# Block-recurrent cross attention and an ELU layer pair on one core: a second Strassen level for P1, softmax steps on GpSimd, later transposes

## The chip, the cores and the metric

One Trainium2 chip, of which the kernel uses one core. The metric is the device time of one execution in microseconds: the median of the runs shown. A core has five instruction queues: PE (TensorE, matmuls, with its weight loads counted apart as PEld), DVE (VectorE), ACT (ScalarE), POOL (GpSimd) and SP (SyncE, here the issuer of nearly all DMAs). Each runs its own queue in order; semaphores tie them together.

## The reference

The inputs are x (8 batches, 8 heads, 512 rows, 64 columns), state (8, 8, 32, 64), w_in (512 by 2048) and w_out (2048 by 512), all float32. Attention goes both ways between x and state, and the result feeds two dense layers with an ELU between them:

```python
scores = scale * np.matmul(x, state.transpose(0, 1, 3, 2))   # softmax over the 32 states -> a
xread = np.matmul(a, state)
scores2 = scale * np.matmul(state, x.transpose(0, 1, 3, 2))  # softmax over the 512 rows -> a2
sread = np.matmul(a2, x)
...
h = x @ w_in                                                 # x: all 4352 rows of [xread, sread]
g = np.where(h > 0.0, h, alpha * (np.exp(np.minimum(h, 0.0)) - 1.0))
return (g @ w_out).astype(np.float32)
```

## The kernel before, in words

**Stages.** Batches 0 and 1 run first (`start()`), while the weights are read and converted; `ffn2_1` ends batch 1; then `batch(b)` runs for b = 2 to 7, and `states()` does the 256 state rows of all batches and the last stores. In the steady part a batch has two halves. The first half is the expansion: four chunks (`ffn1_chunk`) of 512 of the 2048 hidden columns. The transposed softmax weights `a_sb` (128 by 1024) are multiplied with M = state x w_in (`make_m`, from w_in blocks fetched back from DRAM, copied out of PSUM by ACT in `copy_m`). Each chunk is a Strassen-Winograd product: seven products of 128x256 tiles (`two`) instead of eight. Its left sums are made by POOL (`sum_m`), its right sums too (`sum_a`), and `elu` turns the results into `g_sb`. `elu` has two forms: by ACT (exp, relu on ACT, one combining step on DVE) or by DVE (exp on ACT, a tensor_scalar and a max on DVE).

The second half is the contraction g x w_out (`ffn2`), again Strassen-Winograd with seven products P1 to P7. Six of them (P2, P4, P6, P7, P5, P3 in this order) are split once more, by the class `Second`: `sums` makes four sums of g blocks on DVE (128x512 each), and `steps` runs seven products of four 128x128 matmuls each, every one followed by a copy (ACT) or an accumulation (DVE) of a 128x128 block into `ob`. The weight sums of the second level are made once, in `weights`, and `restore` undoes the one of them made in place. P1 alone is plain: 16 matmuls of 128x256 (`product`), and one ACT copy.

**The next batch** is prepared within this one. `load_blocks` brings x of batch b+1 into `ob` (16 DMAs of 64 KB, once `ob`'s former contents are stored), `turn_blocks` transposes it on DVE into `xr` (four instructions of 128x512), `scores` multiplies it with the state. `softmax` makes `a_sb`: transpose, row maximum, subtract, exp, sum, multiply by the reciprocal, transpose. `softmax_rows` makes the weights of the other direction, `move_state` transposes them and moves them across partitions with 16 DMAs, and `state_read` multiplies them with x (`load_x`).

**What sets the order.** Every operation is recorded in a plan (`Plan.add`) with an assumed cost and its dependences. `Plan.run` then goes through the operations engine by engine: PE takes the first ready operation in the written order, the others the ready one that is due first, POOL keeps the written order. DMAs have an assumed rate and landing time (`DMA_COST`, `LANDING`). The order that comes out is fixed in the program. `plan.behind(op)` makes operations wait for `op`, except POOL's. All instructions are issued through one helper, so the profile shows nearly all of them with one line, L463; the groups are told apart by tile names: `ps` is PSUM, `m`, `s` and `aT` hold M and the right factors (and serve as sums' places in the second half), `g` the hidden values, `sec` and `t_w` sums and weights of the second level, `w_half` w_in blocks, `xe` and `xr` the next batch's data, `o` the output and the blocks of the next x.

Of the kernel before, what the change touches and what calls it, by code (L numbers as in the profile page):

```python
# [17 lines left out]
ALU = mybir.AluOpType  # L18
# [3 lines left out]
ENGINES = (POOL, PE, DVE, ACT, SP)  # L22
DMA_COST = {
    "load_w": (0.44, 285e3), "load_w4": (0.44, 370e3), "load_x": (0.6, 270e3), "load_states": (0.6, 75e3),
    "load_blocks": (0.66, 280e3), "move_state": (0.66, 280e3),
}


# [50 lines left out]
class Op:  # L79
    __slots__ = (  # L80
        "number", "engine", "cost", "emit", "deps", "opens", "closes", "port", "moved", "start",
        "end", "due", "users", "name", "instr", "shape", "rank", "rate", "turn", "nudge", "spare",
    )


class Plan:
# [51 lines left out]
    def add(self, engine, cost, emit, ins, outs, port=False, moved=0, tokens=((), ()), name="", shape=None):  # L138
        op = Op()
        op.number, op.engine, op.cost, op.emit = len(self.ops), engine, cost, emit  # L140
        op.deps, op.opens, op.closes, op.port, op.moved = set(), None, [], port, moved
        op.name, op.shape, op.rank, op.rate = name, shape, None, 350e3
        op.nudge, op.spare = 0.0, None
        pieces = []
        banks = {}
        for writes, aps in ((False, ins), (True, outs)):
            for a in aps:
                if isinstance(a, View):
                    banks[id(a.bank)] = a.bank
                else:  # L150
                    pieces.append((writes,) + self.region(a))
        for writes, names in enumerate(tokens):
            for t in names:
                self.writers.setdefault(t, [])
                self.readers.setdefault(t, [])
                pieces.append((bool(writes), t, 1))
        for writes, key, mask in pieces:
            if key is None:
                continue
            for m, o in self.writers[key]:  # L160
                if m & mask:
                    op.deps.add(o)
            if writes:
                for m, o in self.readers[key]:
                    if m & mask:
                        op.deps.add(o)
        for writes, key, mask in pieces:
            if key is None:
                continue
            if writes:  # L170
                self.writers[key] = [
                    (m & ~mask, o) for m, o in self.writers[key] if m & ~mask
                ] + [(mask, op)]
                self.readers[key] = [(m & ~mask, o) for m, o in self.readers[key] if m & ~mask]
            else:
                self.readers[key].append((mask, op))
        for b in banks.values():
            if b.last is None:
                b.first = op
            else:  # L180
                op.deps.add(b.last)
            b.last = op
        op.deps.discard(op)
        self.ops.append(op)
        return op
# [52 lines left out]
    def run(self, until=0.0):  # L238
# [68 lines left out]
        while len(done) < len(self.ops):  # L307
# [40 lines left out]
                port, holds = op.end, e  # L348
            if op.moved:
                wire = max(wire, op.end) + op.moved / op.rate  # L350
                op.end = wire + self.LANDING
                lanes.append(op.end)
            done.append(op)
            for u in op.users:
# [34 lines left out]
def kernel(  # L389
# [154 lines left out]
    def dma(out, in_, tokens=((), ()), queue=SP, kind="dma"):  # L544
        size = 4 * elements(out) * out.shape[0]
        engine = nc.sync if queue == SP else nc.scalar
        cost, rate = DMA_COST.get(kind, (0.44, 370e3))
        op = plan.add(
            queue, cost, issue(engine, "dma_start", dict(out=out, in_=in_)), [in_], [out],
            moved=size, tokens=tokens, name=kind,  # L550
        )
        op.rate = rate

    def bank():
        return Bank(plan).view()
# [158 lines left out]
    def sum_a():  # L714

        r11, r12, r21, r22 = a_blocks_of(a_sb)
        t1, t2, t4 = (a_sb[:, 1024 + 256 * i : 1280 + 256 * i] for i in range(3))
        (V if 0 else Q).tensor_tensor(out=t1, in0=r12, in1=r11, op=ALU.subtract)
        (V if 0 else Q).tensor_tensor(out=t2, in0=r22, in1=t1, op=ALU.subtract)
        (V if 0 else Q).tensor_tensor(out=r12, in0=r22, in1=r12, op=ALU.subtract)  # L720
        (V if 0 else Q).tensor_tensor(out=t4, in0=r21, in1=t2, op=ALU.subtract)

    def a_blocks_of(a):
        return [a[:, g * 512 + j * 256 : g * 512 + (j + 1) * 256] for g in range(2) for j in range(2)]
# [25 lines left out]
    def softmax(b, to):  # L750
        s = st[b, "s"]
        total_t = small(b)[:, 36:68]

        def rows(g):
            return soft_t(b, g).rearrange("p (k n) -> p k n", n=NS)

        for g in range(G):
            V.transpose(out=soft_t(b, g), in_=s[g])
        for g in range(G):
            V.reduce_max(out=tops(b, g)["top_t"], in_=rows(g), axis=AX_X)  # L760
            (V if 3 & 1 and b > 1 or b in [] else Q).tensor_tensor(
                out=rows(g), in0=rows(g), in1=bc(tops(b, g)["top_t"], NS), op=ALU.subtract
            )
            A.activation(out=soft_t(b, g), in_=soft_t(b, g), func=AF.Exp, scale=scale)
            V.reduce_sum(out=tops(b, g)["total_t"], in_=rows(g), axis=AX_X)
        V.tensor_scalar(out=total_t, in0=total_t, scalar1=eps, scalar2=None, op0=ALU.add)
        V.reciprocal(out=total_t, in_=total_t)
        for g in range(G):
            (V if 3 & 2 and b > 1 or b in [] else Q).tensor_tensor(
                out=rows(g), in0=rows(g), in1=bc(tops(b, g)["total_t"], NS), op=ALU.mult  # L770
            )
            V.transpose(out=to[:, g * 512 : (g + 1) * 512], in_=soft_t(b, g))

    def read_weights():
        return xr[:, 1024:].rearrange("p (g r q) -> p g r q", g=G, q=P)

    def turn_state(b):
        for g in range(G):
            ps = bank().rearrange("p (r q) -> p r q", r=R)
            a = soft_a(b, g).rearrange("p (r q) -> p r q", r=R)  # L780
            turns(0.6, [(ps[:, r], a[:, r], ident, {}) for r in range(R)], "turn_state")
            A.copy(out=read_weights()[:, g], in_=ps)

    def move_state(b):
        t = xr[:, :1024]
        for g in range(G):
            V.transpose(out=t[:, g * 512 : (g + 1) * 512], in_=soft_a(b, g))
        t_v = t.rearrange("p (g r q n) -> p g r q n", g=G, r=R, n=NS)
        for m in range(NP):
            for q in range(P // 32):  # L790
                dma(
                    read_weights()[q * 32 : (q + 1) * 32, :, :, m * NS : (m + 1) * NS],
                    t_v[m * 32 : (m + 1) * 32, :, :, q], kind="move_state",
                )

    def state_read(b, at=x_halves):
        ps = bank()
        calls = []
        for g in range(G):
            for r in range(R):  # L800
                for m in range(NP):
                    calls.append((
                        ps[m * NS : (m + 1) * NS, g * D : (g + 1) * D],
                        read_weights()[:, g, r, m * NS : (m + 1) * NS],
                        x_rows(at, r)[:, m * P + g * D : m * P + (g + 1) * D],
                        dict(start=r == 0, stop=r == R - 1, tile_position=(0, m * NS)),
                    ))
# [65 lines left out]
    def ffn1_chunk(b, c, g_to):  # L873
# [14 lines left out]
        def part_1():  # L888
            two(pa, l11, r11, True)
            A.copy(out=pb, in_=pa)  # L890
            two(pc, s1, t1, True)
            two(pb, s2, t2, False)
            two(pa, l12, r21, False)
            A.copy(out=u2, in_=pb)
            elu(pa, g_to[:, k0, lo], e[0], A if c >= 6 - 3 else V)
            two(pb, s3, t3, False)
            A.copy(out=u3, in_=pb)

        def part_2():
# [3 lines left out]
            two(pc, s4, r22, False)  # L903
            elu(pa, g_to[:, k1, hi], e[2], A)
            V.tensor_tensor(out=pc, in0=u2, in1=pc, op=ALU.add)
            elu(pc, g_to[:, k0, hi], e[3], A if c >= 5 - 3 else V)

        return part_1, part_2

# [158 lines left out]
    def store(b, h, o):  # L1068
        rows = out_b[b, 0:S].rearrange("(p r) c -> p r c", r=R)
        dma(rows[:, 2 * h : 2 * h + 2], o.o_sb[h], kind="store")  # L1070

    def words(raw):
        return [raw.rearrange("p n (j w) -> p n j w", w=2)[:, :, :, i] for i in range(2)]
# [196 lines left out]
    def ffn2(o, b):  # L1270
# [3 lines left out]
        spare = spaces(m_sb[:, 1], 3)  # L1274
        o.sum_1()
        late = [plan.ops[-1]]
        if 0:
            second[1].sums(o.a11, spare + s_2[0][:1])
            steps = second[1].steps(c12, fresh=True)
            steps[0]()  # L1280
# [32 lines left out]

        def soft_next():
            if nxt:
                with plan.behind(late[4]):
                    softmax(b + 1, a_sb)
                    softmax_rows(b + 1)
                    load_x(b + 1, x_halves)
# [29 lines left out]
    def ffn2_1(o, b, x1):  # L1349
# [36 lines left out]
            f()  # L1386
        store(b, 1, o)
        second[2].weights(b21)
        if 0: second[1].weights(b11)
        for f in second[3].steps(c12):  # L1390
            f()
        store(b, 0, o)
# [111 lines left out]
    def states():  # L1504
# [7 lines left out]
        for hc in range(5):  # L1512
            fetch_state(hc)
        for k, i in second.items():
            if k > 1 or 0: i.restore()
        xT = st["xT"].rearrange("p m b s -> p m (b s)")
        (r11, r12), (r21, r22) = (
            [xT[:, 2 * k : 2 * k + 2, n * P : (n + 1) * P] for n in range(2)] for k in range(2)
# [98 lines left out]
```

## Time and profile before

| | us |
|---|---|
| median of 3 runs (lowest, highest) | 712.54 (711.35, 713.09) |
| profiled execution | 712.58 |
| its span, first to last instruction | 710.7 |
| PE busy, in matmuls | 695.2 |
| DVE busy | 584.5 |
| ACT busy | 304.9 |
| POOL busy | 113.8 |

The granted TensorE clock was 1.0 over the whole span. The span falls into the start (0 to about 46.7, where DMAs feed the weights), batches 0 and 1 (to about 199, with the second product of batch 1 in the last 40), six batches of 77 to 78 each, and the state rows with the last stores (from about 665). The first half of batch 3 ends near 303, that of batch 4 near 380, of batch 5 near 458, of batch 6 near 535.

How to read the rows: a group's row has the line, the engine, the operation, output and inputs by tile, their form, the count, and then the busy time in us with the mean in ns, the idle time of the engine ahead of it and what ended that. A timeline row has the start in us, the duration, the engine, the operation, a count where equal ones were merged, and in brackets the engine's idle time ahead of it with its releaser. A float32 matmul leaves two records, so a product step of four matmuls shows as x8. Ends of matmuls are modelled and overlap the next one; durations on PE are therefore read from start to start. On DVE, too, consecutive instructions overlap by some 0.08 us: a 128x512 addition lasts 0.68 but the next one starts 0.60 later.

### The profile page before, as it was taken

How to read it: one execution, taken by the hardware profiler on the slowest of the kernel's cores; microseconds unless marked ns; L12 is line 12 of the kernel's file. 1: busy time of each engine (PE TensorE's matmuls, PEld its weight loads, DVE VectorE, ACT ScalarE, POOL GpSimd, SP SyncE). 2: the span in 40 equal slices, each digit the busy share in tenths (PEclk: the TensorE clock that was granted, in tenths of full speed). 3: DMA queues.
4: the chain of work that ended last, by engine and by line, in shares of the span. 5: the costliest groups of instructions: out<-in, count | busy, mean ns of one | idle time of the engine just before them, and what ended most of it. 6: DMA issues, size and time to landing. Idle time of an engine off the chain costs nothing.

```text
span 710.7 us, 14531 instructions
## 1 busy us (share of the span) xinstructions
PE 695.2 (98%) x5802; PEld 589.9 (83%) x5802; DVE 584.5 (82%) x1039; ACT 304.9 (43%) x604; POOL 113.8 (16%) x137
## 2 busy tenths in 40 slices
PE   8899999999999999999999999999999999999996
PEld 7544478889978998789877997799878988899995
DVE  4989999999659996799679994899579976997640
ACT  4989981011066124731275124712374127500630
POOL 1400000022230034100710063002510063000000
PEclk9999999999999999999999999999999999999999
DMA  9677772214270416550482326340664035200300
GB/s 221 197 265 244 272 241 44 59 36 114 90 193 15 120 32 187 110 119 2 93 231 64 61 50 187 91 120 3 186 141 115 5 64 205 60 1 31 119 8 24
DMA packets 132771, 78.54 MB, mean 111 GB/s; under 512 B 113760, under 2 KB 114272, under 8 KB 132704
## 3 DMA queue, kind: packets, MB, share of 16 engines
q1 hardware_dynamic: 130492, 77.06, 39.6%
q8 instruction: 46, 0.75, 0.4%
q10 hardware_dynamic: 2212, 0.56, 0.4%
q14 instruction: 21, 0.17, 0.1%
HBM read 61.34 MB, written 13.11 MB: 105 GB/s over the span
## 4 chain that ended last, share of the span: by engine, by line
PE 82%; DMA 6%; SPq 5%; ACT 2%; DVE 2%; issue 1%; ACTq 0%; DVEq 0%
PE ps L463 82%; SPq L463 5%; DMA w_in_mem<-w_half 2%; DMA o<-in_x_dram 2%; DMA out_dram<-o 1%; DVE g L463 1%; ACT sec L463 1%; DMA xe<-in_x_dram 1%; DMA g<-in_x_dram 1%; DVE ps L463 1%; ACT w_half L463 0%; ACT xe L463 0%; DVE xr L463 0%; ACT o L463 0%; ACTq L463 0%
## 5 line engine op out<-in xcount | busy, mean ns | idle before, releaser
L463 PE MATMUL ps<-aT,m 128*128 128x256 f32 (+1 forms) x568 | 151.2, 408 | 3.6 <-DVE ps L463 1.3
L463 PE MATMUL ps<-w_out,g 128*128 128x128 f32 (+1 forms) x864 | 143.5, 314 | 0.0
L463 PEld LDWEIGHTS ps<-w_out,g 128*128 128x128 f32 x864 | 126.3, 191 | 12.7 <-issue 4.2
L463 PEld LDWEIGHTS ps<-aT,m 128*128 128x128 f32 x568 | 104.2, 190 | 35.7 <-issue 15.9
L463 DVE TENSOR_TENSOR o<-o,ps 128x128 f32<-128x128 f32 (+2 forms) x239 | 67.4, 283 | 43.1 <-PE ps L463 41.5
L463 ACT COPY o<-ps 128x128 f32<-128x128 f32 (+2 forms) x70 | 23.1, 335 | 170.3 <-PE ps L463 164.3
L463 POOL TENSOR_TENSOR m<-m 128x256 f32<-128x256 f32 x72 | 65.9, 939 | 76.6 <-ACT m L463 75.2
L463 POOL TENSOR_TENSOR aT<-aT 128x256 f32<-128x256 f32 x24 | 17.9, 767 | 361.6 <-DVE aT L463 361.2
L463 PE MATMUL ps<-sec 128*128 128x128 f32 x560 | 74.8, 276 | 0.0
L463 ACT ACTIVATE xe<-ps 128x512 f32<-128x512 f32 x96 | 56.2, 597 | 38.5 <-DVE ps L463 21.5
L463 PEld LDWEIGHTS ps<-sec 128*128 128x128 f32 x560 | 68.1, 192 | 2.6 <-DVE sec L463 2.1
L463 PE MATMUL ps<-t_w,s 128*128 128x128 f32 (+1 forms) x432 | 64.7, 299 | 0.0
L463 PEld LDWEIGHTS ps<-t_w,s 128*128 128x128 f32 x432 | 58.4, 192 | 3.7 <-ACT m L463 0.8
L463 DVE SCALAR_TENSOR_TENSOR g<-xe,ps 128x512 f32<-128x512 f32 x66 | 43.9, 681 | 16.2 <-ACT xe L463 16.0
L463 ACT COPY m<-ps 128x512 f32<-128x512 f32 (+1 forms) x56 | 27.1, 534 | 59.6 <-PE ps L463 59.6
L463 PE MATMUL ps<-aT,s 128*128 128x256 f32 x168 | 41.8, 383 | 2.6 <-DVE ps L463 2.4
L463 ACT COPY sec<-ps 128x512 f32<-128x512 f32 (+1 forms) x52 | 29.6, 570 | 30.9 <-PE ps L463 17.4
L463 ACT ACTIVATE xe<-xe 128x512 f32<-128x512 f32 x66 | 40.7, 632 | 1.2
L463 PEld LDWEIGHTS ps<-aT,s 128*128 128x128 f32 x168 | 31.2, 190 | 9.4 <-DVE ps L463 4.0
L463 PE MATMUL ps<-w_half,kT 64*32 64x256 f32 x1024 | 35.9, 382 | 1.5 <-DVE w_half L463 0.9
L463 DVE TENSOR_TENSOR ps<-sec,ps 128x512 f32<-128x512 f32 (+1 forms) x52 | 34.7, 667 | 2.0 <-ACT sec L463 1.0
L463 ACT COPY ps<-ps 128x512 f32<-128x512 f32 (+1 forms) x28 | 15.3, 547 | 45.7 <-PE ps L463 45.7
(152 smaller groups left out, 1147.0 us busy)
## 6 DMA issues: line engine op xcount, KB each, us to landing
w_half<-w_in_mem SPq DMA_DIRECT2D x54, 512.0 KB
t_w<-in_moe_w_out_dram SPq DMA_DIRECT2D x8, 1024.0 KB
t_w<-in_moe_w_in_dram SPq DMA_DIRECT2D x7, 1024.0 KB
out_dram<-o SPq DMA_DIRECT2D x14, 512.0 KB
xe<-in_x_dram SPq DMA_DIRECT2D x26, 256.0 KB
o<-in_x_dram SPq DMA_DIRECT2D x80, 64.0 KB
w_in_mem<-w_half SPq DMA_DIRECT2D x8, 512.0 KB
xr<-xr SPq DMA_DIRECT2D x96, 32.0 KB
```

The source lines that it names most:

```text
L463: ins = getattr(engine, name)(**named)
```

## The change

1. `move_state`, `turn_state`, `read_weights`, `state_read`: the weights of the other direction are laid out by head pair first, so that each of the 16 DMAs moves one run of 256 floats per partition; the DVE transposes and the ACT copies ahead of it write in strides.
2. `softmax`: for batches 2 to 7, too, the subtraction and the multiplication are POOL's. `sum_a`: its four additions are DVE's.
3. `ffn1_chunk`: the first ELU of chunk 2 and the last of chunk 1 are done by ACT's form.
4. `ffn2`: P1 is split by a `Second` like the others; its weight sums are made in `ffn2_1`, and `states()` restores. The order is P1, P2, P4, P6, P7, P5, P3.
5. The softmax of the next batch is held behind the sums of P4 instead of those of P6.
6. The plan's assumptions: x blocks land 1.5 us later, and stores have a rate of 200 GB/s. As the plan sets the order, this moves `turn_blocks` and other instructions in their queues.

```diff
-    "load_blocks": (0.66, 280e3), "move_state": (0.66, 280e3),
+    "load_blocks": (0.66, 280e3, 1.5), "move_state": (0.66, 280e3),
+    "store": (0.44, 200e3),
...
-                op.end = wire + self.LANDING
+                op.end = wire + self.LANDING + op.wait
...
-        (V if 0 else Q).tensor_tensor(out=t1, in0=r12, in1=r11, op=ALU.subtract)
+        (V if 1 else Q).tensor_tensor(out=t1, in0=r12, in1=r11, op=ALU.subtract)
...
-            (V if 3 & 1 and b > 1 or b in [] else Q).tensor_tensor(
+            (V if 0 & 1 and b > 1 or b in [] else Q).tensor_tensor(
                 out=rows(g), in0=rows(g), in1=bc(tops(b, g)["top_t"], NS), op=ALU.subtract
...
-            (V if 3 & 2 and b > 1 or b in [] else Q).tensor_tensor(
+            (V if 0 & 2 and b > 1 or b in [] else Q).tensor_tensor(
                 out=rows(g), in0=rows(g), in1=bc(tops(b, g)["total_t"], NS), op=ALU.mult
...
-        return xr[:, 1024:].rearrange("p (g r q) -> p g r q", g=G, q=P)
+        return xr[:, 1024:].rearrange("p (m g r n) -> p m g r n", m=NP, g=G, n=NS)
...
-        t = xr[:, :1024]
+        t = xr[:, :1024].rearrange("p (q g r n) -> p g r q n", g=G, r=R, n=NS)
         for g in range(G):
-            V.transpose(out=t[:, g * 512 : (g + 1) * 512], in_=soft_a(b, g))
-        t_v = t.rearrange("p (g r q n) -> p g r q n", g=G, r=R, n=NS)
+            V.transpose(
+                out=t[:, g], in_=soft_a(b, g).rearrange("p (r q n) -> p r q n", r=R, n=NS)
+            )
...
-                    read_weights()[q * 32 : (q + 1) * 32, :, :, m * NS : (m + 1) * NS],
-                    t_v[m * 32 : (m + 1) * 32, :, :, q], kind="move_state",
+                    xr[q * 32 : (q + 1) * 32, 1024 + m * 256 : 1280 + m * 256],
+                    xr[m * 32 : (m + 1) * 32, q * 256 : (q + 1) * 256], kind="move_state",
...
-            elu(pa, g_to[:, k0, lo], e[0], A if c >= 6 - 3 else V)
+            elu(pa, g_to[:, k0, lo], e[0], A if c >= 6 - 4 else V)
...
-            elu(pc, g_to[:, k0, hi], e[3], A if c >= 5 - 3 else V)
+            elu(pc, g_to[:, k0, hi], e[3], A if c >= 5 - 4 else V)
...
-        if 0:
+        if 1:
             second[1].sums(o.a11, spare + s_2[0][:1])
             steps = second[1].steps(c12, fresh=True)
             steps[0]()
...
-                with plan.behind(late[4]):
+                with plan.behind(late[3]):
                     softmax(b + 1, a_sb)
...
-        if 0: second[1].weights(b11)
+        if 1: second[1].weights(b11)
...
-            if k > 1 or 0: i.restore()
+            if k > 1 or 1: i.restore()
```

More of the change, by code (lines that the diff above doesn't have):

```diff
@@ L81 @@
         "number", "engine", "cost", "emit", "deps", "opens", "closes", "port", "moved", "start",
-        "end", "due", "users", "name", "instr", "shape", "rank", "rate", "turn", "nudge", "spare",
+        "end", "due", "users", "name", "instr", "shape", "rank", "rate", "turn", "nudge", "spare", "wait",
     )
@@ L142, in add @@
         op.name, op.shape, op.rank, op.rate = name, shape, None, 350e3
-        op.nudge, op.spare = 0.0, None
+        op.nudge, op.spare, op.wait = 0.0, None, 0.0
         pieces = []
@@ L546, in dma @@
         engine = nc.sync if queue == SP else nc.scalar
-        cost, rate = DMA_COST.get(kind, (0.44, 370e3))
+        cost, rate, *wait = DMA_COST.get(kind, (0.44, 370e3))
         op = plan.add(
@@ L551, in dma @@
         )
-        op.rate = rate
+        op.rate, op.wait = rate, sum(wait)
     def bank():
@@ L717, in sum_a @@
         t1, t2, t4 = (a_sb[:, 1024 + 256 * i : 1280 + 256 * i] for i in range(3))
-        (V if 0 else Q).tensor_tensor(out=t1, in0=r12, in1=r11, op=ALU.subtract)
-        (V if 0 else Q).tensor_tensor(out=t2, in0=r22, in1=t1, op=ALU.subtract)
-        (V if 0 else Q).tensor_tensor(out=r12, in0=r22, in1=r12, op=ALU.subtract)
-        (V if 0 else Q).tensor_tensor(out=t4, in0=r21, in1=t2, op=ALU.subtract)
+        (V if 1 else Q).tensor_tensor(out=t1, in0=r12, in1=r11, op=ALU.subtract)
+        (V if 1 else Q).tensor_tensor(out=t2, in0=r22, in1=t1, op=ALU.subtract)
+        (V if 1 else Q).tensor_tensor(out=r12, in0=r22, in1=r12, op=ALU.subtract)
+        (V if 1 else Q).tensor_tensor(out=t4, in0=r21, in1=t2, op=ALU.subtract)
     def a_blocks_of(a):
@@ L781, in turn_state @@
             turns(0.6, [(ps[:, r], a[:, r], ident, {}) for r in range(R)], "turn_state")
-            A.copy(out=read_weights()[:, g], in_=ps)
+            A.copy(
+                out=read_weights()[:, :, g].rearrange("p m r n -> p r m n"),
+                in_=ps.rearrange("p r (m n) -> p r m n", n=NS),
+            )
     def move_state(b):
-        t = xr[:, :1024]
+        t = xr[:, :1024].rearrange("p (q g r n) -> p g r q n", g=G, r=R, n=NS)
         for g in range(G):
-            V.transpose(out=t[:, g * 512 : (g + 1) * 512], in_=soft_a(b, g))
-        t_v = t.rearrange("p (g r q n) -> p g r q n", g=G, r=R, n=NS)
+            V.transpose(
+                out=t[:, g], in_=soft_a(b, g).rearrange("p (r q n) -> p r q n", r=R, n=NS)
+            )
         for m in range(NP):
@@ L803, in state_read @@
                         ps[m * NS : (m + 1) * NS, g * D : (g + 1) * D],
-                        read_weights()[:, g, r, m * NS : (m + 1) * NS],
+                        read_weights()[:, m, g, r],
                         x_rows(at, r)[:, m * P + g * D : m * P + (g + 1) * D],
@@ L1070, in store @@
         dma(rows[:, 2 * h : 2 * h + 2], o.o_sb[h], kind="store")
+        plan.ops[-1].nudge = 0
     def words(raw):
```

## The prediction

> **What bounds the kernel now.** I read the engine totals first, then the chain of waits, then the timeline of TensorE (PE), and last what VectorE (DVE) does just ahead of each gap of PE.
>
> ```profile
> PE 695.2 (98%) x5802; PEld 589.9 (83%) x5802; DVE 584.5 (82%) x1039; ACT 304.9 (43%) x604; POOL 113.8 (16%) x137
> PE 82%; DMA 6%; SPq 5%; ACT 2%; DVE 2%; issue 1%; ACTq 0%; DVEq 0%
> ```
>
> The first line is engine busy time, the second the shares of the chain that ended last. PE is the bound. 15.5 of the 710.7 us are without a matmul: 4.8 in the first 46.7 us, 5.7 after 665 (the last store), the rest in the batches. So time falls only if PE gets less work or its few gaps close. Next the gaps, in PE's timeline and in DVE's for the same place of batch 5:
>
> ```profile
> 442.30 1.03 PE L463 MATMUL ps<-aT,m 128*128 128x256 f32 x4
> 444.36 1.13 PE L463 MATMUL ps<-aT,m 128*128 128x256 f32 x4 [1.03 <-DVE ps L463]
> ...
> 439.91 0.69 DVE L463 TENSOR_TENSOR g<-xe,ps 128x512 f32<-128x512 f32 x1
> 443.00 0.71 DVE L463 STREAM_TRANSPOSE xr<-o 128x512 f32<-128x512 f32 x1 [2.40 <-DMA o<-in_x_dram]
> 443.64 0.67 DVE L463 TENSOR_TENSOR ps<-sec,ps 128x512 f32<-128x512 f32 x1
> ```
>
> PE waits for the addition at 443.64, and that stands in DVE's queue behind a transpose of the next x, which itself waits 2.40 us for the DMA. The same pattern stands in batches 2 to 6. PE's idle times over 0.15 us between 200 and 607 are 0.31, 0.70, 0.16, 0.42, 0.88, 1.03, 0.31, 0.98 = 4.8 us. From start to start each restart loses some 0.16 more (442.30 to 444.36 is 2.06 where the same four records otherwise take 0.86), so the eight cost 6.1 us. Batch 7 loads no next x and has no such gap: that speaks for this cause. The rest of the batch DVE is full but not late:
>
> ```profile
> 340.41 8.35 POOL L463 TENSOR_TENSOR m<-m 128x256 f32<-128x256 f32 x8
> ...
> 332.80 0.68 DVE L463 TENSOR_TENSOR o<-o 128x512 f32<-128x512 f32 x1
> 340.92 1.22 DVE L463 TENSOR_TENSOR o<-o 128x512 f32<-128x512 f32 x1
> ...
> L463 POOL TENSOR_TENSOR sec<-sec 128x512 f32<-128x512 f32 x8 | 10.3, 1308 | 24.8 <-DVE sec L463 24.8
> L463 DVE TENSOR_TENSOR xr<-xr,small 128x512 f32<-128x512 f32 x24 | 16.3, 684 | 0.0
> ```
>
> The same addition takes 0.68 us alone and 1.22 while POOL (GpSimd) runs: that is the price to watch here. The last two are the softmax steps on POOL (batches 0 and 1) and on DVE (batches 2 to 7), and they are what is moved.
>
> **P1 on the second level.** Plain P1 is 16 matmuls of 128x256, 32 records. Eight records of that form run from 362.87 to 364.60, so P1 takes 4 x 1.73 = 6.90 us. A step of the second level is four matmuls of 128x128; consecutive steps start 0.893 apart (313.66, 314.56), and seven take 6.25. That is 0.65 less in each of six batches: **-3.9 us** of PE, the bound itself. DVE pays four sums of 128x512 (starts 0.60 apart, 2.4) and three accumulations (0.20 each, 0.6) per batch; ACT exchanges one copy of 0.59 for four of 0.26. Once, four weight sums (2.4) ahead of batch 1's second product and one restoring sum (0.6) before the state rows. DVE is full from 124 to 185 (15.64 of the first 16 us) with PE never waiting, then waits for PE ten times, 5.5 us in all, up to 197: that takes the sums up; DVE is at 39% in the last 46 us. So both cost 0; without the cover 3.0.
>
> The order of instructions in the changed program shows a second effect: where P1 stood whole behind the last expansion chunk, there are now the first steps of P1, P2, P4 and P6, and the scores stand apart from the make_m block that they followed. Changes between full-array matmuls and the 32-column blocks rise from 60 to 70. One costs about 0.1 us (341.69 to 342.58 is a plain 0.89 step, 340.69 to 341.69 just behind such a block is 1.00). **+1.0 us.**
>
> **The transposes later.** In the changed order the first transpose stands behind the first addition of chunk 1 instead of ahead of it, the others two to five DVE instructions later. At batch 5 the addition would then be ready near 441.4, when ACT's copy for it (from 440.78, 0.58 long) ends, and the transpose takes what is left of the DMA wait behind it. Loads and SP's queue keep their order but for groups of eight and eight instead of seven and nine, so landing hardly moves. I count 85% of 6.1 as won: **-5.2 us**. Ends: 0 (data later by as much as the instructions) and -6.1. What is late next is DVE: from 296 to 313 it has no pause, and P1's sums fall there, the first step on them about 5.5 us of PE work (three other first steps, scores, another two) behind the last chunk. I charge one small restart of 0.25 per batch (the gaps of 0.16 to 0.31 above): **+1.5 us**; ends 0 and +6 (one of about 1 us in each batch).
>
> **Softmax to POOL, sum_a to DVE, two ELUs to ACT.** Per batch DVE loses four steps (2.4) and two tensor_scalars of 0.42 (0.84, in the expansion), and gains the four additions of sum_a, 128x256. DVE has no such row with both inputs in SBUF; between 128x128 (0.20 start to start) and 128x512 (0.60) it is 0.33, so 1.3 (ends 0.8 and 2.4). With P1 the stretch of the second product grows by 2.4 + 0.6 + 1.3 - 2.4 = 1.9 us. POOL exchanges 4 x 0.77 for 4 x 1.31 (alone 1.05, at 25.06; beside DVE up to 1.68); the sums of m queued behind wait no longer for sum_a. The softmax chain is 4 x (1.31 - 0.68) = 2.5 longer; the transposes to aT end at 338.16 and the first matmul on aT starts at 344.37, so 6.2 us hide it. ACT gains 1.26 per batch at 41% load.
>
> Here a rule speaks against the change. Row: beside POOL a two-input addition took +0.54. Rule: "SBUF — State Buffer" (Trainium skill, section "SBUF: two separate sides") says that a DVE instruction with two SBUF inputs and a GpSimd instruction that reads SBUF exclude each other, the later one waiting for the whole of the earlier. By the row, 5.2 us of POOL touch some 3.5 such additions, +1.9 on DVE and 3.8 in all; by the rule up to 5.2, and 7.1 in all. DVE's slack at the end of batch 2's second product is 0.45 + 0.25 + 0.87 + 0.60 + 0.60 + 0.61 + 1.93 = 5.3 us of waiting for PE (265 to 278). The row stays under it, the rule not. I take the row: it was taken at the place itself, where additions were not held for whole POOL instructions. Cost **0**.
>
> **Move of the weights in 1 KB runs.** 16 DMAs per batch, from eight runs of 128 B to one of 1 KB per partition. SP spends 11.0 us issuing them (1.49 + 9.55); the nearest row for long runs is the store, 0.38 each, so 6 to 11 us. state_read starts without a gap in every batch and SP is not the bound: 0. The DVE transposes write strided runs of 32 elements: 0.68 as contiguous (end: double, 1.4 more per batch, off the path); four strided ACT copies in the DMA-fed head, the same. The head's order shifts a little: 0, ends -1 and +1.
>
> **Sum.** The profiled execution took 712.6 (span 710.7 and 1.9 around it), as the median does: 712.6 - 3.9 + 1.0 - 5.2 + 1.5 = **706.0**.
>
> **Rivals.**
> - *A, the sum as it stands:* 704 to 708.5, chance 0.52.
> - *B, all gaps close and nothing new opens:* 712.6 - 3.9 + 1.0 - 6.1 = 703.6 (701.5 to 704). For it: DVE's burst is interleaved with steps whose inputs are ready early. Against: DVE has no pause in that tail even now. 0.20.
> - *C, the transposes do not come late enough, or P1's sums take their place:* the gaps stay by two thirds, 712.6 - 3.9 + 1.0 - 2.0 + 1.5 = 709.2 (708.5 to 711). For it: the first transpose moves past few instructions, and the DMA wait was up to 5.25 us in batch 2; this is the change not doing what it says. 0.19; about a quarter of it lies above 710.4.
> - *D, slower:* GpSimd holds DVE. If the rule's lock applies, DVE grows by 7.1 against 5.3 of slack, and 1.8 per batch reach PE through late evictions and sums: 6 x 1.8 = 10.8, 712.6 - 3.9 + 1.0 - 5.2 + 10.8 = 715.3. It decides from the point where DVE's growth passes 5.3 us per batch. For it: 1.22 against 0.68. Against: POOL already runs 17 us per batch with PE at 98%. 0.07.
> - The remaining 0.02 is no change.
>
> A measurement of this kernel tells 0.3% (2.1 us) from no change. Faster than 710.4: A, B and most of C, 0.89. Same: 0.06. Slower than 714.7: 0.05. The range, 702.3 to 710.0, leaves out the best third of B, C's upper end and D.
>
> **What would show it.** P1: records of 128x256 on w_out,g fall by 192, those of 128x128 rise by 336; a batch on PE is shorter by about 1 us. Transposes: DVE's wait for the x load (14.1 us, 13 times) falls under 5, and PE's gaps behind a DVE addition go. POOL: four xr steps per batch near 1.3 us; DVE's additions beside them under 1.3. Wrong if PE shows gaps ahead of the first step on P1's sums (C), or gaps all through the second product with DVE full and POOL busy (D).

## The result, and the profile after

The changed kernel took **706.09 us**, the median of 4 runs (705.83 to 706.53), beside 712.82 (711.35 to 714.75) for the kernel before: a ratio of 0.9905 with the interval [0.988, 0.9929], so it is faster by about 1%. The forecast was 706.0. That they meet doesn't show that the terms of the sum were right, and two that it had put at 0 were not. The profiled execution took 706.53, its span is 704.4.

First, of the page of the changed kernel, the engine totals, the shares of the chain that ended last, and the row of the softmax steps; then of its groups kept apart by shape the rows that the forecast had named (busy us, mean ns).

```profile
PE 691.7 (98%) x5948; PEld 593.2 (84%) x5948; DVE 591.3 (84%) x1074; ACT 307.4 (44%) x634; POOL 119.8 (17%) x137
PE 13%; DVE 1%; issue 0%; ACT 0%
L464 POOL TENSOR_TENSOR xr<-xr,small 128x512 f32<-128x512 f32 x24 | 27.7, 1176 | 315.9 <-PE ps L464 162.0
```

```profile
L464 PE MATMUL ps<-w_out,g 128*128 128x128 f32 x640 | 84.2, 276 | 0.0
L464 PE MATMUL ps<-w_out,g 128*128 128x256 f32 x128 | 28.6, 379 | 0.0
L464 DVE TENSOR_TENSOR aT<-aT 128x256 f32<-128x256 f32 x24 | 11.2, 487 | 0.0
L464 DVE STREAM_TRANSPOSE xr<-o 128x512 f32<-128x512 f32 x20 | 13.7, 698 | 0.0
```

PE is the bound as before, with 3.5 us less of matmuls. The chain could be followed back over the last 14% of the span only, so nothing is read from it. In the changed kernel's rows the line is L464 where it was L463. The 128x256 records on `w_out,g` went from 320 to 128 and those of 128x128 from 544 to 640, with the rest of P1's steps under `sec` and `t_w`. A softmax step costs POOL 1.18 us on average, and 1.05 alone. The idle time ahead of the transposes is 0.0: the 14.1 us of waiting for the x load are gone. In the timeline of batch 5, the place where PE had lost 1.03 us:

```profile
443.00 0.68 DVE L464 TENSOR_TENSOR m<-g 128x512 f32<-128x512 f32 x1
...
443.59 1.03 PE L464 MATMUL ps<-aT,m 128*128 128x256 f32 x4
443.60 0.68 DVE L464 SCALAR_TENSOR_TENSOR g<-xe,ps 128x512 f32<-128x512 f32 x1
...
444.20 1.30 DVE L464 STREAM_TRANSPOSE xr<-o 128x512 f32<-128x512 f32 x2
...
444.45 1.03 PE L464 MATMUL ps<-aT,s 128*128 128x256 f32 x4
...
445.32 1.03 PE L464 MATMUL ps<-aT,m 128*128 128x256 f32 x4
```

Two transposes stand together, wait for nothing, and PE's groups of four start 0.86 apart without a bracket, which is a group without idle time ahead of it. The gaps that are left are elsewhere (PE's timeline from 200 to 620, all that wait for DVE):

```profile
263.86 1.16 PE L464 MATMUL ps<-sec 128*128 128x128 f32 x8 [0.61 <-DVE o L464]
...
364.02 1.13 PE L464 MATMUL ps<-aT,m 128*128 128x256 f32 x4 [0.16 <-DVE ps L464]
...
489.32 1.16 PE L464 MATMUL ps<-t_w,s 128*128 128x128 f32 x8 [0.56 <-DVE o L464]
...
516.41 1.13 PE L464 MATMUL ps<-aT,m 128*128 128x256 f32 x4 [0.15 <-DVE ps L464]
...
610.94 1.16 PE L464 MATMUL ps<-sec,m 128*128 128x128 f32 x8 [0.59 <-DVE m L464]
```

They come to 2.07, and with 0.16 of slow restart each to 2.9, where it was 6.1. Two of the three large ones lie in the second product, behind additions to `o`. The third, in batch 7, is ahead of the first step on P1's sums (`sec,m`): it waits for the second of these sums, `m<-m,g` at 610.20. Before, all gaps listed were on `aT`, in the expansion.

To see where the time went, the span is cut at two starts that every kernel has: the first matmul of batch 0's second product, and the first of the state rows. "Head" is the time up to the first, "body" from there to the second. Before: head 123.7, body 564.2, rest 22.9. After: 125.1, 557.1, 22.1. So the body gained 7.0, the rest 0.8, and the head lost 1.5.

### The profile page after: what moved, and what is told of

Read it like the earlier page. It is cut to its first block, busy times and chain, and to the rows that moved or that the text cites. A ratio compares the mean times of both kernels' runs of the same rounds, so it can differ in the third digit from the quotient of the medians.

```text
span 704.4 us, 14939 instructions
## 1 busy us (share of the span) xinstructions
PE 691.7 (98%) x5948; PEld 593.2 (84%) x5948; DVE 591.3 (84%) x1074; ACT 307.4 (44%) x634; POOL 119.8 (17%) x137
## 5 line engine op out<-in xcount | busy, mean ns | idle before, releaser
L464 PE MATMUL ps<-aT,m 128*128 128x256 f32 (+1 forms) x568 | 150.3, 408 | 0.6 <-ACT m L464 0.3
L464 PEld LDWEIGHTS ps<-aT,m 128*128 128x128 f32 x568 | 104.5, 190 | 31.8 <-issue 12.3
L464 PE MATMUL ps<-w_out,g 128*128 128x128 f32 (+1 forms) x768 | 112.8, 293 | 0.0
L464 PEld LDWEIGHTS ps<-w_out,g 128*128 128x128 f32 x768 | 102.1, 192 | 9.1 <-issue 4.2
L464 ACT COPY o<-ps 128x128 f32<-128x128 f32 (+2 forms) x88 | 26.0, 299 | 161.1 <-PE ps L464 161.0
L464 DVE TENSOR_TENSOR o<-o,ps 128x128 f32<-128x128 f32 (+2 forms) x257 | 69.7, 281 | 30.8 <-PE ps L464 29.5
L464 POOL TENSOR_TENSOR xr<-xr,small 128x512 f32<-128x512 f32 x24 | 27.7, 1176 | 315.9 <-PE ps L464 162.0
L464 POOL TENSOR_TENSOR m<-m 128x256 f32<-128x256 f32 x72 | 62.8, 893 | 75.4 <-ACT m L464 74.0
L464 PE MATMUL ps<-sec 128*128 128x128 f32 x560 | 74.6, 276 | 0.6 <-DVE o L464 0.6
L464 PEld LDWEIGHTS ps<-sec 128*128 128x128 f32 x560 | 68.5, 192 | 2.8 <-DVE o L464 1.3
L464 PE MATMUL ps<-t_w,s 128*128 128x128 f32 (+1 forms) x432 | 65.4, 299 | 0.7 <-DVE o L464 0.6
L464 ACT ACTIVATE xe<-ps 128x512 f32<-128x512 f32 x96 | 55.1, 603 | 18.1 <-DVE ps L464 11.5
L464 PEld LDWEIGHTS ps<-t_w,s 128*128 128x128 f32 x432 | 58.6, 191 | 4.9 <-ACT m L464 1.3
L464 DVE SCALAR_TENSOR_TENSOR g<-xe,ps 128x512 f32<-128x512 f32 x78 | 51.6, 681 | 8.8 <-ACT xe L464 8.1
L464 ACT COPY m<-ps 128x512 f32<-128x512 f32 (+1 forms) x56 | 27.8, 540 | 62.0 <-PE ps L464 61.9
L464 ACT ACTIVATE xe<-xe 128x512 f32<-128x512 f32 x78 | 47.8, 641 | 0.7
L464 ACT COPY sec<-ps 128x512 f32<-128x512 f32 (+1 forms) x52 | 29.6, 569 | 39.8 <-PE ps L464 33.6
L464 PE MATMUL ps<-aT,s 128*128 128x256 f32 x168 | 41.2, 381 | 0.0
L464 DVE TENSOR_TENSOR ps<-sec,ps 128x512 f32<-128x512 f32 (+1 forms) x52 | 34.8, 669 | 6.2 <-PE ps L464 4.1
L464 PE MATMUL ps<-sec,g 128*128 128x128 f32 (+1 forms) x300 | 37.2, 272 | 1.0 <-DMA g<-in_x_dram 1.0
L464 ACT COPY ps<-ps 128x512 f32<-128x512 f32 (+1 forms) x28 | 15.3, 548 | 51.3 <-PE ps L464 45.1
L464 PEld LDWEIGHTS ps<-aT,s 128*128 128x128 f32 x168 | 31.6, 190 | 5.8 <-issue 1.2
```

The source lines that it names most:

```text
L464: ins = getattr(engine, name)(**named)
```

## The experiments

Times are medians. The runs come in three groups, each on one chip beside the kernel before, to which the ratio is: p1_only to head_before, thin_sums to np_no_wait, and h_soft to np_old_move. The changed kernel's own result stands apart from all three. The kernel before had medians of 713.32, 711.73 and 712.03 in the groups, 1.6 us apart. So between groups a difference of medians under 1.6 us is not read by itself; head and body, each from one profile, are read beside it.

| run | us | ratio, interval | head | body |
|---|---|---|---|---|
| p1_only | 709.35 | 0.9954 [0.994, 0.9968] | 125.8 | 559.6 |
| turns_later | 707.87 | 0.993 [0.9907, 0.9954] | 124.3 | 558.9 |
| no_p1 | 703.27 | 0.9867 [0.9838, 0.9896] | 123.3 | 556.2 |
| head_before | 704.88 | 0.9887 [0.986, 0.9913] | 121.9 | 557.8 |
| thin_sums | 703.89 | 0.9892 [0.987, 0.9913] | 122.8 | 556.8 |
| thin_soft | 702.33 | 0.987 [0.9843, 0.9897] | 122.7 | 555.7 |
| np_soft_dve | 703.21 | 0.9881 [0.9857, 0.9904] | 123.1 | 556.3 |
| np_no_wait | 706.65 | 0.9931 [0.9909, 0.9954] | 122.7 | 560.1 |
| h_soft | 710.85 | 0.9985 [0.9977, 0.9993] | 122.5 | 564.0 |
| h_soft_sum_a | 702.42 | 0.9868 [0.9851, 0.9885] | 122.8 | 555.0 |
| np_elu | 704.46 | 0.9898 [0.9882, 0.9913] | 122.5 | 557.4 |
| np_old_move | 705.23 | 0.9909 [0.9893, 0.9924] | 122.9 | 557.5 |

**p1_only**: the kernel before with P1 on the second level and nothing else.

```diff
-        if 0:
+        if 1:
             second[1].sums(o.a11, spare + s_2[0][:1])
...
-        if 0: second[1].weights(b11)
+        if 1: second[1].weights(b11)
...
-            if k > 1 or 0: i.restore()
+            if k > 1 or 1: i.restore()
```

> The kernel before with P1 on the second level and nothing else. My theory: the matmuls alone pay, 0.65 us in each of six batches, and the gaps behind the x transposes stay: 712.6 - 3.9 = 708.7 (707.5 to 710). PE's records of 128x256 on w_out,g fall by 192. Rival (VectorE cannot carry P1's sums in the tail of the expansion together with the softmax steps): gaps open ahead of the first step on P1's sums and the time is 711.5 or more.

Measured: 709.35, body 4.6 shorter, head 2.1 longer. The 3.9 of matmuls are won in the body (which also still has gaps at the transposes), and a part is given back in the first 125 us. There the change touches no instruction: but the planner, with other work in batches 2 to 7, gives another order there from 19 us on, the same as in the changed kernel. The body also has a new gap in each of its six batches, at the end of the expansion:

```profile
228.16 1.16 PE L463 MATMUL ps<-t_w,g 128*128 128x128 f32 x8 [0.35 <-DVE g L463]
```

It has the size that the forecast gave to a restart (0.25), but waits for one of DVE's last ELU steps, not for P1's sums. The changed kernel doesn't have it.

**turns_later**: the kernel before, with only the four transposes of each next x moved by 1, 3, 3 and 3 DVE instructions, batches 2 to 6; all else in its old order.

```diff
+            if raw is ob:
+                turned.append(plan.ops[-1])
...
+    queue = [op for op in steps if any(op is o for o in turned)]
+    for k, op in reversed(list(enumerate(queue))):
+        at = steps.index(op)
+        n, to = (1, 3, 3, 3)[k % 4], at
+        while n:
+            to += 1
+            other = steps[to]
+            assert op not in other.deps
+            n -= other.engine == DVE and all(other is not o for o in turned)
+        steps.insert(to, steps.pop(at))
+        op.start = steps[to - 1].start
```

> The kernel before, every queue in its old order but for the four transposes of the next x, which stand one, three, three and three VectorE instructions later in batches 2 to 6. My theory: the 6.1 us of restarts in PE go but for about 1: 707.5 (706.5 to 708.5), VectorE's wait for the x load falls from 14.1 to under 5 us. Rival (the data are what is late, so the wait only moves with the instructions): 710.5 or more, and the wait stays over 8 us.

Measured: 707.87, body 5.3 shorter. DVE's wait for the x load falls from 14.1 us to 0.3, once. What stays, in PE's timeline:

```profile
302.30 1.10 PE L463 MATMUL ps<-aT,m 128*128 128x256 f32 x4 [0.57 <-DVE ps L463]
...
378.69 1.10 PE L463 MATMUL ps<-aT,m 128*128 128x256 f32 x4 [0.57 <-DVE ps L463]
...
455.07 1.10 PE L463 MATMUL ps<-aT,m 128*128 128x256 f32 x4 [0.57 <-DVE ps L463]
...
531.46 1.10 PE L463 MATMUL ps<-aT,m 128*128 128x256 f32 x4 [0.57 <-DVE ps L463]
```

The same gap in four batches, now waiting for an addition that is late because DVE's queue ahead of it is full, not because DVE waits. Moving 20 instructions is worth what the forecast said for it (5.2). The listed gaps with their restarts fell from 6.1 to 2.9 only; the other 2 us were lost before in pauses too short to be listed.

**no_p1**: the changed kernel with plain P1, the three flags of p1_only set back to 0.

> The changed kernel with plain P1. My theory (the terms add up): 706.1 + 3.9 = 710.0 (709 to 711). Rival (all of the gain came from the transposes, P1's matmuls were paid back by VectorE): 706 to 707.

Measured: 703.27, **2.8 under the changed kernel** and outside both expected ranges. P1's second level, with the order that the plan gives it, makes the changed kernel slower. Its PE timeline from 200 to 620 has a single gap:

```profile
339.02 1.16 PE L464 MATMUL ps<-sec 128*128 128x128 f32 x8 [0.17 <-DVE o L464]
```

With P1 the body is 0.9 longer, though 3.9 us of matmuls are gone from it, so 4.8 are added. 2.5 of them are the five gaps above against this one. 1.4 lie in the 32-column blocks with the changes into and out of them, read from start to start of PE's records: 74 changes in the body with P1, 64 without it and before, which take the same to 0.01 us. 0.9 are other short pauses. The head is 1.8 longer (125.1 against 123.3): without P1 the planner gives the old order there.

**head_before**: the changed kernel, with the operations of the first 100 us ranked in the order of the kernel before.

```diff
+    for k, n in enumerate(head):
+        plan.ops[n].rank = k
```

> The changed kernel with the operations of the first 100 us in the order that the kernel before gives them. My theory: the changed kernel reaches the same point of batch 0's second product 1.5 us later only because its first 50 us were reordered, so 704.6 (704.0 to 705.3), and the product on t_w,s starts near 123.7 instead of 125.1. Rival (the lower granted clock at 18 to 24 us came by chance or from the changed copies, not from the order): 705.7 to 706.5 and the same start near 125.

Measured: 704.88; head 121.9. The median's 1.2 under the changed kernel would not be enough, but the heads are clear: 121.9 to 124.3 in the twelve profiles with the old order, 125.1 and 125.8 in the two with the new one. So the other order of the head costs about 1 to 3 us, which the forecast had at 0. The gaps of the body stay as they were, with one more of 0.53 in batch 1's second product.

**thin_sums** and **thin_soft**: head_before, every queue in the same order, with P1's four sums, or the softmax steps on POOL, on 8 elements per partition instead of 512. The rest of their work is left out.

```diff
-            def call(**kw):
+            def call(thin=False, **kw):
...
+                if thin:
+                    kw = {k: v[:, :1, :8] if is_ap(v) else v for k, v in kw.items()}
...
-            V.tensor_tensor(out=s1, in0=a21, in1=a22, op=ALU.add)
+            V.tensor_tensor(out=s1, in0=a21, in1=a22, op=ALU.add, thin=self is second[1])
...
-                out=rows(g), in0=rows(g), in1=bc(tops(b, g)["top_t"], NS), op=ALU.subtract
+                out=rows(g), in0=rows(g), in1=bc(tops(b, g)["top_t"], NS), op=ALU.subtract, thin=b > 1
```

> head_before with every queue in its order, but P1's four sums per batch write 8 elements instead of 512 (their values are left out of the result). It takes 2.4 us per batch from VectorE and nothing from PE. My theory: P1's second level pays itself back because its sums use up the slack VectorE had, so PE's gaps (about 3.5 us in head_before) mostly go: 704.9 - 2.2 = 702.7 (702.0 to 703.5). Rival (GpSimd's hold on VectorE alone opens them): 704.2 or more, with the gaps behind VectorE's o additions still there.

> head_before with every queue in its order, but the four softmax steps per batch on GpSimd work on 8 elements instead of 512 (the softmax of batches 2 to 7 is left out so far). GpSimd then holds VectorE 4 us less per batch and the softmax chain is shorter. If the hold decides: the gaps behind o additions go, 704.9 - 1.7 = 703.2 (702.6 to 703.8), and the two-element tensor_scalars on small that lasted up to 1.01 us last 0.16. If VectorE's own load decides: 704.3 or more.

Measured: 703.89 without the work of the sums, between the two expected ranges, and 702.33 without that of the softmax steps, a little under its first. The bodies are 1.0 and 2.1 shorter than head_before's. Thin sums close the gap that waits for `m` (0.59) and leave the two that wait for `o`; thin softmax steps close these two and leave the first. How POOL makes an addition late is read in the timeline of the changed kernel, batch 5, second product:

```profile
486.21 2.31 POOL L464 TENSOR_TENSOR xr<-xr,small 128x512 f32<-128x512 f32 x2 [7.54 <-DVE small L464]
486.54 0.27 DVE L464 TENSOR_TENSOR o<-o,ps 128x128 f32<-128x128 f32 x1
486.73 0.81 DVE L464 TENSOR_SCALAR small<-small 128x2 f32<-128x2 f32 x1
...
487.45 0.27 DVE L464 TENSOR_TENSOR o<-o,ps 128x128 f32<-128x128 f32 x1
...
487.65 1.42 DVE L464 TENSOR_TENSOR sec<-g 128x512 f32<-128x512 f32 x1
...
488.99 0.27 DVE L464 TENSOR_TENSOR o<-o,ps 128x128 f32<-128x128 f32 x1
...
489.32 1.16 PE L464 MATMUL ps<-t_w,s 128*128 128x128 f32 x8 [0.56 <-DVE o L464]
```

and in the same place of thin_soft:

```profile
483.38 0.61 POOL L464 TENSOR_TENSOR xr<-xr,small 128x8 f32<-128x8 f32 x2 [8.62 <-DVE small L464]
483.69 0.27 DVE L464 TENSOR_TENSOR o<-o,ps 128x128 f32<-128x128 f32 x1
483.88 0.16 DVE L464 TENSOR_SCALAR small<-small 128x2 f32<-128x2 f32 x1
...
483.95 0.28 DVE L464 TENSOR_TENSOR o<-o,ps 128x128 f32<-128x128 f32 x1
...
484.15 1.07 DVE L464 TENSOR_TENSOR sec<-g 128x512 f32<-128x512 f32 x1
485.14 0.27 DVE L464 TENSOR_TENSOR o<-o,ps 128x128 f32<-128x128 f32 x1
```

Two elements per partition take 0.81 us instead of 0.16: they wait until POOL's first step ends, near 487.5. The addition of 512 behind it ends at 489.07, which is the end of POOL's second step, 488.52, and 0.55: it too was held for the rest of a POOL instruction. (In thin_soft it takes 1.07 and not 0.68, since a sum of `m` on POOL, ending at 484.67, holds it: again it ends 0.55 later.) The additions `o<-o,ps`, which read PSUM, are not held themselves (0.27 both times), but stand behind the held ones. From the tensor_scalar to the last addition it is 2.26 us against 1.26, and PE waits for that addition.

**np_soft_dve**: no_p1 with the softmax steps back on DVE.

```diff
-            (V if 0 & 1 and b > 1 or b in [] else Q).tensor_tensor(
+            (V if 3 & 1 and b > 1 or b in [] else Q).tensor_tensor(
...
-            (V if 0 & 2 and b > 1 or b in [] else Q).tensor_tensor(
+            (V if 3 & 2 and b > 1 or b in [] else Q).tensor_tensor(
```

> no_p1 with the softmax steps on VectorE as before. My theory: moving them to GpSimd gave VectorE 2.4 us per batch back, and that is most of the 2.7 us by which no_p1's part from 123 us on is shorter than turns_later's: 705.5 (704.5 to 706.5). Rival (what VectorE gained it lost by waiting for GpSimd): 702.8 to 703.8.

Measured: 703.21 beside no_p1's 703.27. The bodies are 556.3 and 556.2. So without P1's sums the place of the softmax steps is worth nothing. DVE's slack in all does not tell why. Ahead of the additions to `o` DVE waits for PE 50.7 us in no_p1 and 32.6 in the changed kernel; but it is 35.0 in np_soft_dve, which has no gap over 0.24, and 38.0 in thin_sums, which keeps both gaps. So what counts is the order at the place; which part of it lets no_p1 escape was not tested.

**np_no_wait**: no_p1 without the assumption that x blocks land 1.5 us later, which is what moves the transposes in the plan.

```diff
-    "load_blocks": (0.66, 280e3, 1.5), "move_state": (0.66, 280e3),
+    "load_blocks": (0.66, 280e3), "move_state": (0.66, 280e3),
```

> no_p1 without the 1.5 us by which the plan takes the x blocks to land later. My theory: the transposes stand early again, VectorE waits for the load by more than 6 us in all, and PE's gaps return: 703.3 + 4 = 707 (705.5 to 708.5). Rival (the other changes moved the queues enough): 703 to 704.5 and a wait under 4.

Measured: 706.65, 3.4 over no_p1, with a body 3.9 longer, and the wait is back. A line has the waiting engine and tile, the releaser, and then us in all, times, and the longest; first no_p1, then np_no_wait:

```profile
DVE xr L464 <- DMA o<-in_x_dram: 1.5, 1, 1.5
```

```profile
DVE xr L464 <- DMA o<-in_x_dram: 13.7, 11, 2.0
```

So one assumed number in the plan carries about 3.4 of what no_p1 gains.

**h_soft**: head_before with the softmax steps on DVE (the edit of np_soft_dve), sum_a staying on DVE. **h_soft_sum_a**: sum_a back on POOL as well, which is the division of the kernel before.

```diff
-        (V if 1 else Q).tensor_tensor(out=t1, in0=r12, in1=r11, op=ALU.subtract)
+        (V if 0 else Q).tensor_tensor(out=t1, in0=r12, in1=r11, op=ALU.subtract)
```

(and its three other additions likewise)

> head_before with the softmax steps of batches 2 to 7 on VectorE. If GpSimd's hold costs more than the 2.4 us per batch that VectorE takes on: the gaps behind o additions go and the time is 703.0 (702.3 to 703.8). If VectorE, which now carries P1's sums and the softmax, is the limit: gaps ahead of P1's steps and 705 to 707.

> h_soft with sum_a on GpSimd again, so that of the moves between VectorE and GpSimd none is left and P1, the later transposes, the ELUs, the 1 KB runs and the old head remain. My theory: VectorE has 1.3 us per batch more, GpSimd runs sum_a where it disturbs only transposes: 702.3 (701.5 to 703.2), at or under no_p1. Rival: P1's extra block changes and gaps stay, 703.5 or more.

Measured: 710.85, over both expected ranges, and 702.42. With P1's sums, the softmax steps and sum_a all on DVE, PE waits in more places. From one state_read to the next, batches take 75.9, 78.9, 78.6 and 81.8, and gaps come in both halves of the batch, two of which are these in h_soft's PE timeline:

```profile
530.92 2.04 PE L464 MATMUL ps<-aT,m 128*128 128x256 f32 x8 [0.68 <-ACT sec L464]
534.34 1.16 PE L464 MATMUL ps<-t_w,s 128*128 128x128 f32 x8 [1.38 <-DVE g L464]
```

DVE's busy time doesn't tell the two apart (597.7 and 598.3), though in the second DVE is held longer by POOL (14.8 us against 9.9, counted as in the next section). With sum_a on POOL and the softmax on DVE, the time is 2.5 and the body 2.8 under head_before's, as much as thin_soft won by leaving the work out. So the exchange of these two, with the order that the plan makes of it, was a loss for a kernel with P1 on the second level; the plan also moves most of DVE's other instructions, so work and order are not separated here. This is the best version that leaves nothing out, 3.7 under the changed kernel; from no_p1 (0.8, in another group) it isn't told apart.

**np_elu**: no_p1 with the two ELUs back on DVE. **np_old_move**: no_p1 with the weights of the other direction laid out and moved as before.

```diff
-            elu(pa, g_to[:, k0, lo], e[0], A if c >= 6 - 4 else V)
+            elu(pa, g_to[:, k0, lo], e[0], A if c >= 6 - 3 else V)
...
-            elu(pc, g_to[:, k0, hi], e[3], A if c >= 5 - 4 else V)
+            elu(pc, g_to[:, k0, hi], e[3], A if c >= 5 - 3 else V)
```

```diff
-                    xr[q * 32 : (q + 1) * 32, 1024 + m * 256 : 1280 + m * 256],
-                    xr[m * 32 : (m + 1) * 32, q * 256 : (q + 1) * 256], kind="move_state",
+                    read_weights()[q * 32 : (q + 1) * 32, :, :, m * NS : (m + 1) * NS],
+                    t_v[m * 32 : (m + 1) * 32, :, :, q], kind="move_state",
```

> no_p1 with the two ELUs in VectorE's form again. turns_later shows one gap of 0.57 us in each of four batches behind a VectorE addition at the end of the expansion; no_p1 has none. If the 0.84 us that the two ELUs save VectorE there closed them: 703.3 + 2.5 = 705.8 (705.0 to 706.5) with gaps of that kind. If the new order closed them: 703 to 704.

> no_p1 with the weights of the other direction laid out and moved as before, in 128 B runs. My theory: nothing waits for these DMAs, 703.3 within 0.6. Rival: the long runs let state_read start earlier or relieve SP: 704.5 or more, with gaps ahead of state_read.

Measured: 704.46 (+1.2, and the body +1.2) and 705.23 (+2.0, the body +1.3). np_elu lies between what the two theories expected, with gaps of 0.17 to 0.27 only. np_old_move has the size that the rival gave, but not the gap ahead of state_read that would go with it; its one gap is behind an addition (0.50). Its order changed with the plan, so that the DMAs themselves cost 2.0 is not shown. In the changed kernel the 16 issues of a batch take SP 10.1 to 10.8 us where it was 11.5 to 12.0 (all but the first batch), so little is saved there; the packets fell from 132,771 to 111,270.

## Why the prediction was right in sum, and where it was wrong

Added up from start to start of PE's records, the body's 7.0 us are: -3.9 matmuls, +1.4 changes of blocks, -3.2 listed gaps with their restarts (6.1 to 2.9), -1.3 shorter pauses. The last stage gave 0.8 more and the head took 1.5. The forecast had no term for the pauses and the last stage, and 0 for the head: that these cancel is luck.

- **P1, -3.9**: right for the matmuls, by the records and by the body of p1_only. But in the changed kernel P1 is a net loss of 2.8 (no_p1), 1.8 of it in the head. The work of its sums on DVE, which the forecast set against 5.3 us of slack per batch, is a part of the rest only: 1.0 of body in the same order (thin_sums), most of it the gap named under the restarts.
- **Changes of blocks, +1.0**: right in kind and a little low; ten more changes, 1.4 in the changed kernel. In p1_only six of the ten fall on the gaps of 0.35, so it can't be told there.
- **Transposes, -5.2**: right in mechanism (turns_later -5.3; the wait 14.1 to none). The size is in part luck: 3.2 of turns_later's 5.3 are the gaps that the forecast counted, the rest are pauses that it didn't count.
- **Restarts, +1.5**: near in size, the place right once. The gap ahead of the first step on P1's sums came in one batch of six, 0.59, and with the two small gaps on `aT` and the restarts it makes 1.4. The other 1.5 of the 2.9 are behind additions to `o`, and belong to the next term.
- **GpSimd, "I take the row", 0**: failed, at about 2 (body of thin_soft 2.1, median 2.6 under head_before's). The rule of "SBUF — State Buffer" (Trainium skill, section "SBUF: two separate sides"), which the forecast set aside, has the mechanism: the held DVE instruction waits for the rest of POOL's, and not only with two inputs from SBUF, as the tensor_scalar of one shows. The section also names DVE's two-port modes; whether this tensor_scalar runs in one, no run here shows.
- **Head, 0 (ends -1 and +1)**: failed at +1.5, outside its ends. Reading it needed the changed order of this stretch, not only the operations changed.
- **What no term had**: without P1 the rest of the change shortens the body by 8.0, 2.7 more than the transposes. It is about the size of the four gaps of 0.57 with their restarts (2.9) that turns_later has and no_p1 has not. Setting back the ELUs loses 1.2 of body, setting back the layout 1.3, but neither brings these gaps back. These are sizes of the plan's whole order with and without them, not of single instructions. The earlier softmax and the assumed rate of the stores (5 and 6 of the change) were not set back alone.

The row that the forecast took against the rule is itself such a hold. In the kernel before, around the addition of 1.22:

```profile
340.41 1.18 POOL L463 TENSOR_TENSOR m<-m 128x256 f32<-128x256 f32 x1
340.92 1.22 DVE L463 TENSOR_TENSOR o<-o 128x512 f32<-128x512 f32 x1
```

POOL's instruction ends at 341.59 and the addition at 342.14, 0.55 later, as above. Between 200 and 664 us all 30 additions of 128x512 without a PSUM operand that last over 0.8 in that trace end 0.53 to 0.57 after an instruction of POOL. So "not held for whole POOL instructions" misread the row: an addition was held for as long as POOL's instruction still ran.

The sum drawn from the rule, 10.8, was too high by four or five times. It let the softmax steps hold DVE for up to 5.2 us per batch. Take as held every DVE instruction without a PSUM operand that lasts over 0.1 us more than the median of its shape in the trace (0.16 for two elements): from 200 to 664 us all of them, in every trace, run beside POOL. In the changed kernel the softmax steps hold seven instructions for 3.4 us, in six batches together. All holds come to 13.5 us in the kernel before, 12.7 in the changed kernel, and 14.8 in h_soft_sum_a, which is faster. So neither their sum nor a batch's slack, against which the forecast set rule and row, tells what they cost. What decides is what stands directly behind the held instruction, and when PE needs that.

Rival A had the time, by a mixture that it did not describe. Of D the mechanism is real, at a fifth to a quarter of its price. C's gaps at the transposes did not stay, and its gap at P1's sums came once; nor did all gaps close (B). The chance of "faster" was also added up wrongly: A, B and three quarters of C make 0.86, not 0.89.

## What to carry to other kernels

Where one engine is 98% busy, taking work off it pays only while what feeds it comes in time at the very place: here 3.9 us of matmuls brought 4.8 us of gaps, block changes and short pauses with them, about 2 of which GpSimd's holds caused, and with this division of work the kernel was better without. A hold by GpSimd is to be priced at the instruction queued behind the held one, not against a batch's slack. And where a planner sets the order, changing one flag moves instructions far from it: separate the order from the work (old order with new work, same order with thin work) before crediting either.

## What the runs showed of the chip that was not expected

The granted clock was halved once in the head of two of the profiles. Busy time in stretches of 3.41 us (columns: the stretch, its length, busy PE, PEld, DVE, ACT and POOL with instructions, then the granted clock, DMA share, GB/s), first the changed kernel, then turns_later:

```profile
15.01:18.42 3.41, 1.93 (x32) 1.46 (x28) 3.41 (x9) 2.21 (x4) 0.96 (x1) 1.00 1.10 315
18.42:21.83 3.41, 3.41 (x34) 2.44 (x38) 3.40 (x9) 1.30 (x3) 1.58 (x2) 0.50 0.97 332
```

```profile
16.90:20.31 3.41, 1.99 (x26) 1.62 (x24) 3.41 (x10) 1.84 (x5) 0.61 (x1) 1.00 1.04 367
20.31:23.72 3.41, 3.33 (x24) 1.44 (x23) 2.94 (x5) 2.69 (x7) 1.89 (x2) 0.50 0.50 192
```

In both, the clock was 0.50 for 3.41 us, and in the 3.41 us ahead of that PE, waiting for x blocks, had been busy 1.93 and 1.99. Cut every trace up to 690 us into such steps, counted from where it first notes the clock: these two are the least busy of all fourteen runs. The next ones, 2.02 (the changed kernel, from 32.08) and 2.04 (h_soft, from 531.58), kept 1.00. Where a stretch begins matters: from 15 to 18 us PE was busy only 1.64 in thin_soft, and the clock stayed at 1.00. "TensorE: Matmul & The Clock Gate" (Trainium skill, Part 1) has the clock halved after an idle window of about 3.4 us. The length agrees, but by an idle window neither trace should have dipped; here one busy for 57 to 58% was enough.

In the changed kernel eight fill matmuls (L1581, there only to keep PE busy) took 2.08 us there instead of 1.16, and the scores 1.58 instead of 1.09: some 1.4 us. The dip isn't what made the head longer, for p1_only has the same order, no dip, and a head of 125.8.
